# Batch 1's exp(q) transposed in quarters of the array, in one block ahead of its first kv

## The chip, the cores and the metric

One core of one Trainium2 chip. The metric is the device time of one execution in microseconds (us), the median of several runs; lower is better. A ratio given here is the mean time of one kernel's runs over that of the other's of the same rounds, so it is not quite the ratio of the medians that stand beside it.

## The reference

```python
# q, k, v: (8 batches, 8 heads, 576 rows, 64)
q_s = softmax(q, axis=-1)                  # over the 64
k_s = softmax(k, axis=2)                   # over the 576 rows
kv  = einsum('bhsd,bhse->bhde', k_s, v)        # 64 x 64 per head
x   = einsum('bhsd,bhde->bhse', q_s, kv)   # -> (4608, 512)
out = gelu(x @ w_in) @ w_out               # w_in 512x2048, w_out 2048x512
```

## The kernel before

TensorE does the matmuls and transposes, VectorE, ScalarE and GpSimd the work on single elements (exp, sums, casts, copies), and SyncE's queue issues nearly all of the loads. TensorE writes its results into banks of PSUM, from where VectorE or ScalarE copies them. TensorE works through the batches: transposes of exp(q), kv, x, then the two large products h (with w_in) and y (with w_out). Batch 1's attention is laid into the y stage of batch 0, which runs in 16 steps t of four matmuls each; step t needs row block t of w_out, cast to bf16.

```python
def tp_mm(b, half):                 # 8 full 128x128 transposes
    ...
    for i in range(2):
        hp = 2 * half + i
        for j in range(J):
            nc.tensor.transpose(ps[:, j, i, :], <eq of two heads, 128 x 128>, identity)

def norm_q(b, i=0, n=1, eng=None):  # half of the heads: sum, reciprocal, product
    ...
    nc.vector.reduce_sum(out=qsum, in_=eq[:, :, hs, :], axis=AX.X)
    nc.vector.reciprocal(recq, qsum)
    eng.tensor_tensor(out=eq[...], in0=eq[...], in1=<recq>, op=ALU.mult)
...
load_main(1, "q", q, 2)             # one queue, in this order
load_pair(1, "k", k, 2)
wo.append(load_wo(3))               # rows 12 and 13 of w_out
for hp in range(2):
    load_v1(hp)
load_wo_row(wo[3], 2)               # rows 14, 15
load_wo_row(wo[3], 3)
load_v1(2)
load_v1(3)
...
exp_q(1, parts=2)                   # ScalarE
exp_k(1, parts=2)
...
norm_q(1, 0, 2)                     # product on GpSimd
norm_q(1, 1, 2, nc.vector)          # product on VectorE
cast_wo(3, wo[3], 0, 2)             # rows 12 and 13, VectorE
for hp in range(HP):
    cast_v(1, hp, nc.gpsimd)
for t in range(12):
    y_part(t, range(J))
tp_step(1, 0)                       # transposes, copies on VectorE
tp_step(1, 1)
load(3)
cast_wo(3, wo[3], 2, 1, "s")        # row 14, ScalarE
cast_wo(3, wo[3], 3, 1, "s")        # row 15
y_part(12, range(J))
y_part(13, range(J))
kv_mm(1, 0)                         # 36 matmuls in 64x64 quarters
kv_norm(1, 0)
y_part(14, range(J))
y_part(15, (0, 1))
...
x_mm(1, 0)                          # 4 matmuls in quarters
kv_mm(1, 1)
```

The softmax here doesn't subtract the row's maximum and nothing guards it: scores larger than these inputs give would overflow.

Of the kernel before, what the change touches and what calls it, by code (L numbers as in the profile page):

```python
# [9 lines left out]
BF16 = mybir.dt.bfloat16  # L10
# [6 lines left out]
def kernel(  # L17
# [16 lines left out]
    nc = tc.nc  # L34
# [3 lines left out]
    J = 4  # L38
    M = 128 * J
    R = S - M  # L40
    HP = H // 2
# [8 lines left out]
    attn_sb = ctx.enter_context(tc.tile_pool(name="attn_sb", bufs=2))  # L50
    small = ctx.enter_context(tc.tile_pool(name="small", bufs=4))
    moe_sb = ctx.enter_context(tc.tile_pool(name="moe_sb", bufs=4))
    psum_h = ctx.enter_context(tc.tile_pool(name="psum_h", bufs=3, space=bass.MemoryType.PSUM))
    psum_y = ctx.enter_context(tc.tile_pool(name="psum_y", bufs=2, space=bass.MemoryType.PSUM))
    psum_a = ctx.enter_context(tc.tile_pool(name="psum_a", bufs=1, space=bass.MemoryType.PSUM))

    identity = singles.tile([128, 128], BF16)
# [20 lines left out]
    def table(func):  # L78
        nc.scalar.activation(out=scr[:, 1:2], in_=scr[:, 0:1], func=func)  # L79

    st = [dict() for _ in range(B + 1)]
# [30 lines left out]
    def load(b):  # L112
        load_main(b, "q", q)
        load_pair(b, "k", k)
        load_pair(b, "v", v)
# [52 lines left out]
    def kv_tiles(b):  # L168


        if b == 0:
            p = [psum_h.tile([128, 512], FP32, tag="h", name="kv")[:, 0:256] for i in range(2)]
            ps = psum_a.tile([128, 4, 256], FP32, tag="a2", name="kv")
            st[b]["kvall"] = ps[:, 0::2]
            p += [ps[:, 0, :], ps[:, 2, :]]
        else:
            ps = psum_a.tile([128, 4, 256], FP32, tag="a2", name="kv")
            st[b]["kvall"] = ps
            p = [ps[:, i, :] for i in place]
        st[b]["kv"] = p  # L180
# [7 lines left out]
    def kv_mm(b, half):  # L188


        if "kv" not in st[b]:
            kv_tiles(b)
        for n in range(NS):
            for i in range(2):
                for hh in range(2):
                    hp = 2 * half + i
                    pr = slice(hh * 64, hh * 64 + 64)
                    c = slice((hh ^ i) * 64, (hh ^ i) * 64 + 64)
                    nc.tensor.matmul(  # L199
                        st[b]["kv"][hp][c, 0:D + 1], ek[b % 2][pr, hp, n, :],  # L200
                        v_aug[b % 2][pr, hp, n, 0:D + 1], start=(n == 0), stop=(n == NS - 1),
                    )

    def kv_norm(b, half=None):

        ps = st[b]["kvall"]
        if half is None:
            parts = [(ps, kvc[b], 4)]
        elif b == 0 and half == 0:
            parts = [(st[b]["kv"][hp].unsqueeze(1), kvc[b][:, hp:hp + 1], 1) for hp in range(2)]  # L210
        elif b == 0:
            parts = [(ps, kvc[b][:, 2:4], 2)]
        else:
            parts = [(ps[:, 1:3] if half == 0 else ps[:, 0::3], kvc[b][:, 2 * half:2 * half + 2], 2)]
        for src, dst, m in parts:
            rec = small.tile([128, 4], FP32, tag="reck")
            nc.vector.reciprocal(rec[:, 0:m], src[:, :, D])
            nc.vector.tensor_tensor(  # L218
                out=dst, in0=src[:, :, 0:D],
                in1=rec[:, 0:m].unsqueeze(2).to_broadcast([128, m, D]), op=ALU.mult,  # L220
            )
# [6 lines left out]
    def norm_q(b, i=0, n=1, eng=None):  # L228

        eng = eng or nc.gpsimd  # L230
        eq = st[b]["eq"]
        w = H // n
        hs = slice(i * w, (i + 1) * w)
        qsum = small.tile([128, J, w], FP32, tag="qsum")
        recq = small.tile([128, J, w], FP32, tag="recq")
        nc.vector.reduce_sum(out=qsum, in_=eq[:, :, hs, :], axis=AX.X)  # L236
        nc.vector.reciprocal(recq, qsum)  # L237
        eng.tensor_tensor(  # L238
            out=eq[:, :, hs, :], in0=eq[:, :, hs, :],
            in1=recq.unsqueeze(3).to_broadcast([128, J, w, D]), op=ALU.mult,  # L240
        )

    def tp_mm(b, half):
        if half == 0:
            st[b]["qT"] = attn_sb.tile([128, J, HP, 128], BF16, tag="qT", name="qT")
        if b == 1 and half == 1:
            ps = psum_a.tile([128, 2, J, 2, 128], BF16, tag="a2", name="tp")[:, 0]
        else:
            pool, tag = (psum_h, "h") if half == 1 else (psum_a, "a")
            ps = pool.tile([128, J, 2, 128], BF16, tag=tag)  # L250
        st[b][f"tp{half}"] = ps
        for i in range(2):
            hp = 2 * half + i
            for j in range(J):
                nc.tensor.transpose(  # L255
                    ps[:, j, i, :],
                    st[b]["eq"][:, j, 2 * hp:2 * hp + 2, :].rearrange("p h d -> p (h d)"),
                    identity,
                )

    def tp_evac(b, half, eng="v"):
        o = st[b]["qT"][:, :, 2 * half:2 * half + 2, :]
        if eng == "v":
            nc.vector.tensor_copy(out=o, in_=st[b][f"tp{half}"])
        else:
            nc.scalar.copy(out=o, in_=st[b][f"tp{half}"])

    def tp_step(b, half):
        tp_mm(b, half)
        tp_evac(b, half)  # L270

    def xbar_step(b):
        st[b]["qT"] = attn_sb.tile([128, J, HP, 128], BF16, tag="qT", name="qT")
# [80 lines left out]
    def y_mm(c, ps, j, t):  # L354
        nc.tensor.matmul(  # L355
            ps, st[c]["g"][:, t, j * 128:(j + 1) * 128], wo_bf[:, t, :],
            start=(t == 0), stop=(t == NDF - 1),
        )
# [83 lines left out]
    def load_wo(i):  # L442
        w = wst.tile([128, 4, DM], FP32, tag="w")
        src = moe_w_out[i * 512:(i + 1) * 512, :]
        if i == 0:
            for h in range(2):
                nc.sync.dma_start(
                    out=w[:, 2 * h:2 * h + 2],
                    in_=src[256 * h:256 * h + 256].rearrange("(p c) f -> p c f", c=2),
                )  # L450
            return w
        src = src.rearrange("(p c) f -> p c f", c=4)
        if i == 3:
            nc.sync.dma_start(out=w[:, 0:2], in_=src[:, 0:2])
            return w
        nc.sync.dma_start(out=w, in_=src)
        return w
# [5 lines left out]
    def cast_wo(i, w, c0=0, n=4, eng="v"):  # L463
        o, w = wo_bf[:, 4 * i + c0:4 * i + c0 + n, :], w[:, c0:c0 + n]
        if eng == "v":
            nc.vector.tensor_copy(out=o, in_=w)
        else:
            nc.scalar.copy(out=o, in_=w)
# [18 lines left out]
    wo = [load_wo(i) for i in range(3)]  # L487
# [19 lines left out]
    norm_q(0, 0, 2)  # L507
    norm_q(0, 1, 2, nc.vector)
    tp_mm(0, 0)
    cast_v(0, 0, nc.scalar)  # L510
    cast_v(0, 1, nc.scalar)
# [3 lines left out]
    x_tile(0, 0, psum_y, "y")  # L515
    x_tile(0, 1, psum_y, "y")
    tp_mm(0, 1)
    tp_evac(0, 1, "s")
    x_tile(0, 2, psum_a, "a")
# [40 lines left out]
    exp_k(1, parts=2)  # L560
    table(AF.Gelu)
    cast_wo(2, wo[2])
    yps = [psum_h.tile([128, DM], FP32, tag="h", name="ps") for j in range(2)]
    yps += [psum_y.tile([128, DM], FP32, tag="y", name="ps") for j in range(2)]
    norm_q(1, 0, 2)
    norm_q(1, 1, 2, nc.vector)
    cast_wo(3, wo[3], 0, 2)
    for hp in range(HP):
        cast_v(1, hp, nc.gpsimd)

    def y_part(t, js):
        for j in js:
            y_mm(0, yps[j], j, t)

    for t in range(12):
        y_part(t, range(J))
    tp_step(1, 0)
    tp_step(1, 1)
    load(3)
    cast_wo(3, wo[3], 2, 1, "s")  # L580
    cast_wo(3, wo[3], 3, 1, "s")
    y_part(12, range(J))
    y_part(13, range(J))
    kv_mm(1, 0)
    kv_norm(1, 0)
    y_part(14, range(J))
    y_part(15, (0, 1))
# [110 lines left out]
```

## Time and profile before

| | before |
|---|---|
| time, median | 279.49 us (279.39 to 279.51, 3 runs) |
| TensorE busy | 97% of 277.7 us |
| granted clock | 0.998 |
| DMA engines, first 48.6 us | busy for nine tenths or more in six of the seven slices of 6.9 us, at 397 to 429 GB/s |

The table says: TensorE's stream sets the time, and for nearly all of the first 48 us the loads keep the DMA engines full beside it.

### The profile page before, as it was taken

How to read it: one execution, taken by the hardware profiler on the slowest of the kernel's cores; microseconds unless marked ns; L12 is line 12 of the kernel's file. 1: busy time of each engine (PE TensorE's matmuls, PEld its weight loads, DVE VectorE, ACT ScalarE, POOL GpSimd, SP SyncE). 2: the span in 40 equal slices, each digit the busy share in tenths (PEclk: the TensorE clock that was granted, in tenths of full speed). 3: DMA queues.
4: the chain of work that ended last, by engine and by line, in shares of the span. 5: the costliest groups of instructions: out<-in, count | busy, mean ns of one | idle time of the engine just before them, and what ended most of it. 6: DMA issues, size and time to landing. Idle time of an engine off the chain costs nothing.

```text
span 277.7 us, 4535 instructions
## 1 busy us (share of the span) xinstructions
PE 269.6 (97%) x1890; PEld 126.3 (45%) x1918; DVE 100.7 (36%) x154; ACT 157.8 (57%) x246; POOL 32.4 (12%) x26
## 2 busy tenths in 40 slices
PE   7899999999999999999999999999999999999995
PEld 3444454444444444444444444444444444444443
DVE  2876574319753540093008400751015200130012
ACT  4867675789377717791669246943683363126400
POOL 1520051002020220004000500050005000000000
PEclk9999999999999999999999999999999999999999
DMA  7999999964992248712981199017401500220033
GB/s 254 397 401 429 399 400 407 400 245 107 305 328 59 75 104 256 288 38 91 251 340 40 47 254 380 34 46 193 112 0 76 151 2 0 76 78 0 0 78 77
DMA packets 44980, 50.10 MB, mean 180 GB/s; under 512 B 20384, under 2 KB 29856, under 8 KB 44704
## 3 DMA queue, kind: packets, MB, share of 16 engines
q1 hardware_dynamic: 44560, 49.39, 53.0%
q10 hardware_dynamic: 400, 0.43, 0.6%
q8 instruction: 15, 0.25, 0.4%
q14 instruction: 5, 0.04, 0.1%
HBM read 36.70 MB, written 9.44 MB: 166 GB/s over the span
## 4 chain that ended last, share of the span: by engine, by line
PE 93%; DMA 4%; issue 1%; POOL 0%; DVE 0%; SPq 0%
PE ps L327 44%; PE ps L355 43%; DMA f<-in_v_dram 2%; PE kv L199 2%; PE ps L294 2%; DMA f<-in_q_dram 1%; PE ps L380 1%; PE pair L327 1%; POOL v_aug L162 0%; PE ps L299 0%; PE tp L255 0%; PE ps L255 0%; SPq L103 0%; DVE kvc L218 0%; DVE y_sb L385 0%
## 5 line engine op out<-in xcount | busy, mean ns | idle before, releaser
L327 PE MATMUL ps<-xT,wi_bf 128*128 128x512 bf16 x557 | 124.2, 379 | 0.5
L355 PE MATMUL ps<-wo_bf,g 128*128 128x512 bf16 x543 | 122.1, 379 | 1.6 <-issue 1.1
L333 ACT ACTIVATE g<-ps 128x512 bf16<-128x512 f32 x142 | 83.5, 598 | 66.8 <-PE ps L327 66.8
L327 PEld LDWEIGHTS <-wi_bf 128*128 128x128 bf16 x576 | 56.1, 98 | 68.0 <-POOL wi_bf L440 0.2
L355 PEld LDWEIGHTS <-g 128*128 128x128 bf16 x560 | 53.8, 98 | 64.4 <-issue 0.4
L363 DVE COPY y_sb<-ps 128x512 f32<-128x512 f32 x33 | 22.6, 684 | 82.1 <-PE ps L355 79.1
L238 POOL TENSOR_TENSOR e<-e,recq 128x2048 bf16<-128x2048 bf16 (+1 forms) x9 | 25.7, 2855 | 176.3 <-DVE recq L237 141.7
L162 DVE CAST v_aug<-f 128x576 bf16<-128x576 f32 x24 | 16.4, 745 | 47.6 <-DMA f<-in_v_dram 47.6
L236 DVE TENSOR_REDUCE qsum<-e 128x16 f32<-128x1024 bf16 (+1 forms) x13 | 21.1, 1622 | 14.2 <-ACT e L145 14.2
L320 ACT CAST xT<-ps 128x512 bf16<-128x512 f32 x18 | 9.9, 588 | 28.4 <-PE ps L294 18.3
L145 ACT ACTIVATE e<-f 128x512 bf16<-128x512 f32 (+1 forms) x42 | 20.5, 556 | 3.3 <-DMA f<-in_q_dram 3.2
L150 ACT ACTIVATE ek<-f 128x2304 bf16<-128x2304 f32 (+1 forms) x10 | 17.2, 1728 | 0.7 <-DMA f<-in_k_dram 0.7
L318 DVE CAST xT<-ps 128x512 bf16<-128x512 f32 x17 | 11.0, 686 | 16.8 <-PE ps L294 14.0
L79 ACT ACT_TABLE_LOAD x9 | 11.5, 1283 | 2.8 <-issue 2.6
L473 PE MATMUL ps<-zeros 128*128 128x512 f32 x14 | 9.0, 814 | 1.5 <-DVE zeros L498 1.5
L145 ACT ACT_TABLE_LOAD x7 | 9.0, 1283 | 0.1
L199 PEld LDWEIGHTS <-ek 64*64 64x64 bf16 x576 | 6.5, 105 | 2.7 <-issue 1.0
L432 DVE CAST wi_bf<-w 128x512 bf16<-128x512 f32 x12 | 6.9, 616 | 1.9 <-DMA w<-in_moe_w_in_dram 1.6
L199 PE MATMUL kv<-v_aug,ek 64*64 64x65 bf16 x576 | 7.0, 193 | 0.5 <-POOL v_aug L162 0.5
L473 PEld LDWEIGHTS ps<-zeros 128*128 128x128 f32 x14 | 3.6, 269 | 6.0 <-issue 4.5
L238 DVE TENSOR_TENSOR e<-e,recq 128x1024 bf16<-128x1024 bf16 x4 | 6.2, 1550 | 0.1
L294 PE MATMUL ps<-qT,kvc 64*64 64x512 bf16 x62 | 5.4, 390 | 0.5 <-DVE kvc L218 0.4
(38 smaller groups left out, 49.8 us busy)
## 6 DMA issues: line engine op xcount, KB each, us to landing
out_dram<-y_sb SPq DMA_DIRECT2D x32, 256.0 KB, 2.4
f<-in_k_dram SPq DMA_DIRECT2D x6, 1152.0 KB, 10.2
f<-in_v_dram SPq DMA_DIRECT2D x6, 1152.0 KB, 11.6
f<-in_q_dram SPq DMA_DIRECT2D x6, 1024.0 KB, 7.0
w<-in_moe_w_in_dram SPq DMA_DIRECT2D x6, 512.0 KB, 8.4
f<-in_v_dram SPq DMA_DIRECT2D x8, 288.0 KB, 6.5
f<-in_q_dram SPq DMA_DIRECT2D x4, 512.0 KB, 8.8
w<-in_moe_w_out_dram SPq DMA_DIRECT2D x2, 1024.0 KB, 12.1
```

The lines of the kernel that those rows point to most:

```text
L79: nc.scalar.activation(out=scr[:, 1:2], in_=scr[:, 0:1], func=func)
L145: nc.scalar.activation(out=dst[:, i], in_=src[:, u], func=AF.Exp)
L150: nc.scalar.activation(out=ek[b % 2][:, i:i + n], in_=st[b]["kf"][:, i:i + n].rearrange("p x (n d) -> p x n d", n=NS), func=AF.Exp,)
L162: eng.tensor_copy(out=o, in_=i)
L199: nc.tensor.matmul(st[b]["kv"][hp][c, 0:D + 1], ek[b % 2][pr, hp, n, :], v_aug[b % 2][pr, hp, n, 0:D + 1], start=(n == 0), stop=(n == NS - 1),
L236: nc.vector.reduce_sum(out=qsum, in_=eq[:, :, hs, :], axis=AX.X)
L238: eng.tensor_tensor(out=eq[:, :, hs, :], in0=eq[:, :, hs, :], in1=recq.unsqueeze(3).to_broadcast([128, J, w, D]), op=ALU.mult,)
L327: nc.tensor.matmul(ps, wi_bf[:, dm, t * 128:(t + 1) * 128], st[c]["xT"][:, dm, :], start=(dm == 0), stop=(dm == NDM - 1),)
L333: nc.scalar.activation(out=st[c]["g"][:, t, :], in_=ps, func=AF.Gelu)
L355: nc.tensor.matmul(ps, st[c]["g"][:, t, j * 128:(j + 1) * 128], wo_bf[:, t, :], start=(t == 0), stop=(t == NDF - 1),)
L363: nc.vector.tensor_copy(out=y_sb, in_=ps)
L473: nc.tensor.matmul(ps, z[:, 0:128], z, start=True, stop=True)
```

## The change

Its intent: the transposes are made in the four quarters of the array, as kv is, and put next to kv, so that both form one block in one tiling mode. Each half of the partitions gets its own PSUM bank; VectorE copies one, ScalarE the other. Since y step 12 now comes before the transposes, the cast of row 12 is split from row 13's. (The diff is cut; left out is also the branch of tp_mm that gave the old second tile its bank.)

```diff
+    def tp_quarters(b, tps):
+        for hp in range(HP):
+            for j in range(J):
+                for hh in range(2):
+                    for r in range(2):
+                        pr = slice(r * 64, r * 64 + 64)
+                        nc.tensor.transpose(
+                            tps[r][hh * 64:hh * 64 + 64, hp, j, :],
+                            st[b]["eq"][pr, j, 2 * hp + hh, :], identity[pr, pr],
+                        )
+    def tp_quarters_evac(b, tps, r, eng):      # cut: one copy on VectorE or ScalarE
...
+    tps = [pool.tile([128, HP, J, 64], BF16, tag=tag, name="tp")
+           for pool, tag in ((psum_a, "a"), (psum_h, "h"))]
...
-    cast_wo(3, wo[3], 0, 2)
+    cast_wo(3, wo[3], 0, 1)
+    cast_wo(3, wo[3], 1, 1)
...
-    tp_step(1, 0)
-    tp_step(1, 1)
     load(3)
...
     y_part(12, range(J))
     y_part(13, range(J))
+    tp_quarters(1, tps)
     kv_mm(1, 0)
+    tp_quarters_evac(1, tps, 0, "v")
+    tp_quarters_evac(1, tps, 1, "s")
     kv_norm(1, 0)
```

More of the change, by code (lines that the diff above doesn't have):

```diff
@@ L245, in tp_mm @@
             st[b]["qT"] = attn_sb.tile([128, J, HP, 128], BF16, tag="qT", name="qT")
-        if b == 1 and half == 1:
-            ps = psum_a.tile([128, 2, J, 2, 128], BF16, tag="a2", name="tp")[:, 0]
-        else:
-            pool, tag = (psum_h, "h") if half == 1 else (psum_a, "a")
-            ps = pool.tile([128, J, 2, 128], BF16, tag=tag)
+        pool, tag = (psum_h, "h") if half == 1 else (psum_a, "a")
+        ps = pool.tile([128, J, 2, 128], BF16, tag=tag)
         st[b][f"tp{half}"] = ps
@@ L266, in tp_evac @@
             nc.scalar.copy(out=o, in_=st[b][f"tp{half}"])
-    def tp_step(b, half):
-        tp_mm(b, half)
-        tp_evac(b, half)
+    def tp_quarters(b, tps):
[9 more added lines that the diff above has]
+    def tp_quarters_evac(b, tps, r, eng):
+        if r == 0:
+            st[b]["qT"] = attn_sb.tile([128, J, HP, 128], BF16, tag="qT", name="qT")
+        o = st[b]["qT"].rearrange("p j x m -> p x j m")[:, :, :, r * 64:r * 64 + 64]
+        if eng == "v":
+            nc.vector.tensor_copy(out=o, in_=tps[r])
+        else:
+            nc.scalar.copy(out=o, in_=tps[r])
     def xbar_step(b):
```

## The prediction

> **What bounds the kernel now.** I first read the busy shares and the heads of the chain of waits on the page, to see which engine's time is the kernel's time.
>
> ```profile
> PE 269.6 (97%) x1890; PEld 126.3 (45%) x1918; DVE 100.7 (36%) x154; ACT 157.8 (57%) x246; POOL 32.4 (12%) x26
> ...
> PE 93%; DMA 4%; issue 1%; POOL 0%; DVE 0%; SPq 0%
> ```
>
> TensorE is busy 97% of the 277.7 us span and holds 93% of the chain that ended last; the 4% of DMA lie in the first 11 us. The granted clock is 0.998. So from 12.7 us on, time taken from TensorE's stream comes off the end one for one, as long as no other engine becomes late by it.
>
> Next I read the chain of waits in order of time around batch 1's front end, which the change touches. Columns: start in us, length in us, what. A piece runs from the end of the work before it to its own end, so its length is what it adds to the chain.
>
> ```profile
> 38.44 0.45 PE ps L255 x8
> 38.89 0.45 PE tp L255 x8
> 39.34 1.73 PE ps L355 x8
> 41.06 0.41 PE kv L199 x36
> 41.47 0.32 PE ps L355
> 41.79 0.05 issue
> 41.85 1.02 PE ps L355 x4
> 42.87 0.34 PE ps L294 x4
> 43.21 0.34 PE kv L199 x34
> 43.55 0.54 PE ps L355 x2
> ```
>
> L255 are the transposes of exp(q), L355 the output matmuls (y), L199 kv, L294 the attention product x. There is no wait in it: 16 full transposes add 0.90 us (56 ns each), eight y matmuls 1.73 (216 each), the first half of kv 0.41.
>
> The same chain, near its end, holds the one block that is nearly the new one's shape: 64 matmuls of 64x64 weights and 64 columns, entered from full-array matmuls.
>
> ```profile
> 241.80 0.67 PE ps L299 x64
> ```
>
> Last I read the timeline of ScalarE, VectorE and GpSimd in the same stretch, for the slack of what will stand after the transposes. Columns: start, length, engine, line, operation.
>
> ```profile
> 39.73 1.28 ACT L468 CAST wo_bf<-w 128x512 bf16<-128x512 f32 x2 [0.82 <-DMA w<-in_moe_w_out_dram]
> 43.26 0.58 ACT L320 CAST xT<-ps 128x512 bf16<-128x512 f32 x1 [2.25 <-PE ps L294]
> ...
> 36.22 1.68 DVE L238 TENSOR_TENSOR e<-e,recq 128x1024 bf16<-128x1024 bf16 x1
> 37.82 0.68 DVE L466 CAST wo_bf<-w 128x1024 bf16<-128x1024 f32 x1
> ...
> 39.53 0.68 DVE L264 COPY qT<-tp 128x1024 bf16<-128x1024 bf16 x1
> 41.54 0.17 DVE L217 RECIPROCAL rec<-kv 128x2 f32<-128x2 f32 x1 [1.32 <-PE kv L199]
> 41.74 0.29 DVE L218 TENSOR_TENSOR kvc<-kv,rec 128x128 bf16<-128x128 f32 x1
> ```
>
> ScalarE stands idle from 41.01 to 43.26 and VectorE from 40.21 to 41.54: the two copies of the new order have room there.
>
> **What the Trainium skill says.** "TensorEngine Tiling (Array Packing)", section Key Properties: tiles of one mode run independently and in parallel, but a change of the mode drains the engine. The trace agrees in size: 36 kv matmuls entered from full-array work add 0.41 us, 36 that follow x in the same mode add 0.34, so entry costs about 0.07. The same page, section Gotcha 1: row tiles must not write one PSUM bank at the same time; the change gives each half of the partitions its own bank. "TensorE: Matmul & The Clock Gate", Part 4, tells of some 275 ns for a transpose in a kernel, with the full clock not engaging. The trace has 219 ns for one, but 56 ns from one to the next, so in a stream they run at the full rate; the measurement decides. "VectorE: DVE Perf Modes", section Mode 2x_1P, says that 16-bit elements go two per cycle where neighbours are packed and aligned. The trace agrees: 1024 bf16 out of PSUM took 0.68 us, as long as 512 fp32 (the y_sb copies, 0.68).
>
> **The change part by part.**
>
> Removed: 16 full transposes ahead of y step 12, 0.90 us on the chain.
>
> Added: 64 transposes of 64x64, right ahead of the first kv. With kv they form one block in one mode, so no mode change is added: the entry moves from kv to the transposes. Steady rate in this mode: 36 kv in 0.34 us are 9.4 ns each, and the x block of 64 gives (0.67 - 0.07)/64 = 9.4. So the block costs 64 x 9.4 + 0.07 = 0.67 us, the measured length of L299, and the kv after it loses its entry: 0.34 instead of 0.41. I chose these as models because operand sizes, the alternation of row halves and the 64-column stream are nearly the same; what is untested is the transpose mode.
>
> Sum on TensorE, from the end of y step 11 to the end of kv: before 0.90 + 1.73 + 0.41 = 3.04 us; after 1.73 + 0.67 + 0.34 = 2.74. **A gain of 0.30 us.**
>
> Moved, and whether it stays hidden (times shifted by that gain):
> - y step 12 now follows step 11 directly, at 38.44 instead of 39.34, and needs row 12 of w_out. That cast is split in two. Casts of this kind cost (1.23 - 0.68)/1024 = 0.54 ns an element, so one row takes about 0.40 us and, started at 37.82, is ready near 38.25. The first matmul of step 12 enters the array about 38.25 (its piece ends 216 ns after 38.44). A tie, worth 0.1 us at most; unsplit, the cast would have cost about 0.3. The second row, near 38.65, has till 39.1.
> - Transposes then end near 40.84 and kv near 41.18. VectorE copies one half from 40.9 to about 41.6 (0.69), then the reciprocal and product (0.46): kv is normalised near 42.1. The x matmuls start about 42.3 (their piece, now 42.57 to 42.91, less some 0.3 for their own passage). Slack 0.2 us.
> - ScalarE ends its two casts at 41.01 and copies the other half in about 1.01 us, the time of the one such copy it made for batch 0: done near 42.05. Slack again some 0.25 us. The x products now need both copies, where they needed VectorE's alone.
> - PSUM banks: the built program gives the second transpose tile the bank that the last GELU of the stage before frees; the first y matmuls keep their banks and waits, so allocating it earlier blocks nothing.
> - kv's second half needs two v casts of GpSimd that end at 42.44; it would start at 42.9. Hidden.
>
> Everything later is the same stream 0.30 us earlier.
>
> **The rivals.**
> 1. A new wait takes the gain. The copies now stand between the transposes and x with only 0.2 us to spare. VectorE's writes change to runs of 64 elements; should this halve its rate, 1024 elements would take about 0.68 + 512 x 1.04 ns = 1.2 us (slope my estimate, twice the 0.54 of the casts less fixed cost), kvc comes near 42.6 and x waits some 0.3: time unchanged, near 279.5. For it: slack is small. Against: runs of 64 remain packed.
> 2. The transposes do not overlap between quarters. At a full-array rate for 64 columns, half the 56 ns, 64 take 1.8 us, 1.1 more than planned, and the copies end later too: about 280.5. For it: no transpose in this trace runs in quarters. Against: kv and x do, with nearly the same shape and bank pattern.
> 3. The gain is hidden anyway, because a load or cast sets a later start. The DMA engines are full in this stretch (some 390 to 410 GB/s), and w_out's last rows and batch 1's v land just ahead of their use. Against: after 12.7 us the chain has no DMA in it, and slack of the nearest, GpSimd's v casts, is 0.5 us. It would leave 279.3 to 279.5.
>
> **Range and chances.** 279.49 - 0.30 = 279.19; a little of rivals 1 and 3 and the tie of step 12 bring it to 279.2. The runs before lie within 0.12 us. The low end, 278.95, is the gain plus noise and a somewhat faster block; the high end, 279.6, holds a gain wholly eaten and noise. I give the overlap about nine chances in ten. Two per cent is 5.6 us, which nothing here comes near: within 2% at 0.98, 0.01 to either side.
>
> **What the changed profile would show.** Right: in the chain, y steps 10 to 13 unbroken, then 64 transposes in about 0.67 us and 36 kv in 0.34 with no issue gap between; the x matmuls near 42.57 without a wait; VectorE's copy still near 0.7 us, ScalarE's near 1.0. Wrong: a piece of VectorE or ScalarE (qT, kvc) in the chain before x means rival 1; transposes adding 25 ns or more each, rival 2; a DMA or GpSimd piece after 43 us, rival 3. A wait of y step 12 on the w_out cast would show the tie lost. A time above 279.6 means that one of them took more than the whole gain.

## More of the kernel before

The timeline of TensorE (start, length, engine, line, work, and in brackets the idle time before it with what ended it):

```profile
27.92 10.52 PE L355 MATMUL ps<-wo_bf,g 128*128 128x512 bf16 x47
```

```profile
31.98 1.24 ACT L145 ACTIVATE e<-f 128x512 bf16<-128x512 f32 x3 [1.97 <-DMA f<-in_q_dram]
```

TensorE begins y at 27.92; twelve steps of four matmuls at 0.216 us each are fed to it till 38.28, where the transposes start. ScalarE waits for batch 1's q and begins its exp when it lands, at 31.98. VectorE does two sums, two reciprocals, one product and then the cast of rows 12 and 13. In this kernel nothing on TensorE needs that cast before 39.17.

## The result, and the profile after

| | before | changed |
|---|---|---|
| time, median | 279.53 us (279.39 to 279.65, 6 runs) | 279.57 us (279.24 to 279.88, 6 runs) |
| span of the profiled run | 277.7 us | 277.7 us |

The ratio is 1.0002, interval 0.9989 to 1.0015: the same time. The forecast gain of 0.30 us did not come. Parts of the chain of waits of the changed kernel, from the load of q to x, say where it went; lines of the source have moved by 14 (y is L369, x L308), and the new transposes are L272.

```profile
19.80 12.47 DMA f<-in_q_dram
...
36.50 1.70 DVE e L238
38.20 0.35 DVE wo_bf L480
38.55 0.04 issue
38.59 1.89 PE ps L369 x8
40.47 0.64 PE tp L272 x64
41.11 0.35 PE kv L199 x33
...
42.87 0.34 PE ps L308 x4
```

Before, the chain kept to TensorE from 12.7 us on, but for 0.5 us of VectorE at 13.2 us and the last copy. Now it runs back from y step 12 over VectorE's cast of row 12, its product on exp(q), the sums and the exp to the load of q, and TensorE enters it only at 38.59. The block that was built is there and costs what was forecast: 64 transposes 0.64 us and kv 0.35. The timeline of TensorE shows the wait itself.

```profile
27.76 10.52 PE L369 MATMUL ps<-wo_bf,g 128*128 128x512 bf16 x47
38.59 1.89 PE L369 MATMUL ps<-wo_bf,g 128*128 128x512 bf16 x8 [0.30 <-DVE wo_bf L480]
```

The account closes. In this execution y began at 27.76, 0.16 earlier than in the trace of before. Twelve steps of four matmuls take 10.36 us (27.92 to 38.28 in the trace of before), so step 12 could have started at 38.12; it started at 38.59, 0.47 late. (The 0.30 in the bracket counts from the modelled end of the last matmul, which lies past the end of its feed.) The block's own saving, against the four pieces of before, is 0.45 + 0.45 + 1.73 + 0.41 - (1.73 + 0.64 + 0.35) = 0.32. And 0.16 + 0.32 - 0.47 is nothing: x starts at 42.80 in both traces. Why the cast was late, the timelines of ScalarE and VectorE tell; the first line of each is what came of q's landing, the second the new copy.

```profile
32.29 1.24 ACT L145 ACTIVATE e<-f 128x512 bf16<-128x512 f32 x3 [2.43 <-DMA f<-in_q_dram]
...
41.20 1.01 ACT L284 COPY qT<-tp 128x1024 bf16<-128x1024 bf16 x1
```

```profile
38.12 0.75 DVE L480 CAST wo_bf<-w 128x512 bf16<-128x512 f32 x2
41.17 0.69 DVE L282 COPY qT<-tp 128x1024 bf16<-128x1024 bf16 x1 [2.30 <-PE tp L272]
```

q landed 0.31 us later than in the trace of before (32.29 against 31.98), and everything behind it shifted by as much. SyncE's queue, which issues the loads in order, tells where these 0.31 us come from (before, then changed):

```profile
19.51 1.59 SPq L90 DMA_DIRECT2D f<-in_q_dram  x2
```

```profile
19.80 1.60 SPq L90 DMA_DIRECT2D f<-in_q_dram  x2
```

The load of q was issued 0.29 us later. From issue to the start of the exp it took 12.47 and 12.49 us, as good as the same. So the load itself was not slower; it started later. What it waited for, by the chain, is a load of w_in that landed at 19.78.

The two copies took 0.69 and 1.01 us as forecast, and x did not wait for them.

### The profile page after: what moved, and what is told of

The parts are those of the page before. It is cut to its first block, busy times and chain, and to the rows that moved or that the text cites. A ratio compares the mean times of both kernels' runs of the same rounds, so it can differ in the third digit from the quotient of the medians. Undisturbed runs are those within 1.5% of the kernel's fastest.

```text
span 277.7 us, 4630 instructions
## 1 busy us (share of the span) xinstructions
PE 269.1 (97%) x1938; PEld 126.0 (45%) x1966; DVE 100.6 (36%) x154; ACT 158.9 (57%) x247; POOL 32.5 (12%) x26
## 4 chain that ended last, share of the span: by engine, by line
PE 84%; DMA 11%; DVE 2%; issue 1%; ACT 0%; SPq 0%
PE ps L369 40%; PE ps L341 40%; DMA f<-in_q_dram 6%; DMA w<-in_moe_w_in_dram 3%; DMA f<-in_v_dram 2%; PE kv L199 2%; PE ps L308 1%; PE ps L394 1%; DVE qsum L236 1%; DVE e L238 1%; ACT e L145 0%; PE ps L313 0%; PE tp L272 0%; DVE recq L237 0%; DVE wo_bf L480 0%
## 5 line engine op out<-in xcount | busy, mean ns | idle before, releaser
L369 PE MATMUL ps<-wo_bf,g 128*128 128x512 bf16 x543 | 122.1, 379 | 1.9 <-issue 1.1
L369 PEld LDWEIGHTS <-g 128*128 128x128 bf16 x560 | 54.0, 98 | 65.0 <-issue 1.0
L308 PE MATMUL ps<-qT,kvc 64*64 64x512 bf16 x62 | 5.6, 390 | 0.3 <-DVE kvc L218 0.2
```

The costliest lines, as they stand in the source:

```text
L369: nc.tensor.matmul(ps, st[c]["g"][:, t, j * 128:(j + 1) * 128], wo_bf[:, t, :], start=(t == 0), stop=(t == NDF - 1),)
```

## The experiments

**Theories.** A: the gain on TensorE is real, and y step 12, moved forward, turns it into a wait for the cast of row 12, which stands on VectorE behind its work on q and so hangs on the landing of q. B: the loads hold the whole stretch, so that without this wait the next one takes its place. C: the late landing was chance, and typical runs do gain. The kernels ran in three groups, each on one chip beside nine common runs of before: after_again, skip_row12, one_cast and early_row12 (before: 279.49 us, 279.39 to 279.59); moved_full, quarters_early, before_early and early_v_act (279.61, 279.42 to 280.01); before_again, pool_norm and early_v_again (279.54, 279.35 to 279.68). Each kernel was timed five times.

| run | median, us | ratio to before | 95% interval |
|---|---|---|---|
| before_again | 279.55 | 0.9999 | 0.9986 to 1.0011 |
| after_again | 279.55 | 1.0004 | 0.9991 to 1.0016 |
| skip_row12 | 279.18 | 0.9994 | 0.9981 to 1.0006 |
| one_cast | 280.14 | 1.0021 | 1.0009 to 1.0034 |
| early_row12 | 279.34 | 0.9992 | 0.9978 to 1.0006 |
| moved_full | 279.87 | 1.0007 | 0.9994 to 1.0019 |
| quarters_early | 279.38 | 0.9989 | 0.9976 to 1.0003 |
| before_early | 279.79 | 1.0008 | 0.9995 to 1.0020 |
| early_v_act | 279.22 | 0.9988 | 0.9976 to 1.0001 |
| early_v_again | 279.21 | 0.9987 | 0.9973 to 1.0000 |
| pool_norm | 280.11 | 1.0023 | 1.0010 to 1.0035 |

Only the intervals of one_cast and pool_norm, both slower, leave out 1. That a kernel here is faster than before by 0.1 to 0.4 us is shown by its trace, not by the times.

### The two kernels again: before_again and after_again

No edit (a comment at the end of the file).

> The kernel before against itself: how far two sets of runs of one kernel differ (expected: ratio within 0.0005 of 1), and a second trace of it: the cast of rows 12 and 13 again done well ahead of step 12 (by 0.5 us or more), no wait of TensorE between 30 and 43 us, or at most one of the second half of the transposes on VectorE's product when q lands late.

> The changed kernel once more, as control and as a second look at how late the loads are. Theory A (the gain of 0.30 us on TensorE is eaten by y step 12, which now waits for the cast of row 12 of w_out at the end of VectorE's work on batch 1's q): same time as before within 0.1 us, about 279.5, and again a VectorE piece for the cast ahead of y step 12 in the chain, 0.1 to 0.5 us of wait depending on when q lands. Theory C (the first runs had late loads by chance): 279.2 and no wait.

Measured: before against itself gives 0.9999, so no offset between two sets of runs shows here, though the interval is ten times that. Its second trace again has no wait, and the cast of rows 12 and 13 ended at 38.45, 0.78 us ahead of its step 12. The changed kernel's second trace has y begun at 27.92, so that step 12 could start at 38.28; it started at 38.62, 0.34 late, again behind VectorE's cast. With two traces of two that have the wait, and medians of 279.57 and 279.55, theory C falls: single runs may gain (279.24 and 279.32 are among the eleven), the typical one does not.

### Step 12 without its cast: skip_row12

```diff
-            ps, st[c]["g"][:, t, j * 128:(j + 1) * 128], wo_bf[:, t, :],
+            ps, st[c]["g"][:, t, j * 128:(j + 1) * 128],
+            wo_bf[:, 11 if c == 0 and t == 12 else t, :],
```

Its output is wrong, which doesn't matter for the time. Relative error 0.12: step 12 uses a row that was cast long before.

> Wrong result on purpose: y step 12 of batch 0 multiplies by row block 11 of w_out, cast long before, so that it has no cast to wait for; every instruction and duration is kept. Theory A: y steps 11, 12, 13 unbroken, time 0.3 us below before, about 279.2. Theory B (the loads hold this stretch in several places, and the next wait takes over: step 13's row, the normalised exp(q), v's casts or rows 14 and 15): time stays at 279.5 and the chain shows another VectorE, GpSimd or ScalarE piece before 43 us.

```profile
32.88 7.34 PE ps L369 x34
40.22 0.64 PE tp L272 x64
40.85 0.35 PE kv L199 x35
41.21 1.40 PE ps L369 x6
42.61 0.34 PE ps L308 x4
```

The chain of waits is one unbroken run of y matmuls, and x is done 0.26 us earlier than before's (x began at 42.54, against 42.80) although y began 0.04 later. (By the 6.3 us that step 12 follows the start of the exp in the changed kernel, 38.59 - 32.29, its cast would here have let it start near 38.5, with the exp at 32.19, some 0.2 after TensorE was ready.) The median is 279.18, 0.31 below before. Four of the five runs lie between 279.14 and 279.24; the fifth took 279.88, which no trace explains and which alone brings the ratio up to 0.9994. Theory A holds, and B does not, as far as this wait goes.

### A longer cast: one_cast

```diff
-    cast_wo(3, wo[3], 0, 1)
-    cast_wo(3, wo[3], 1, 1)
+    cast_wo(3, wo[3], 0, 2)
```

> The changed kernel with the cast of rows 12 and 13 in one instruction again, as before the change. Theory A: step 12 waits until the whole cast, 0.68 instead of 0.41 us, is done: 0.3 us more wait, time about 279.8. If the cast were not what holds the end: no change, 279.5.

```profile
32.78 1.25 ACT e L145 x3
...
38.69 0.62 DVE wo_bf L480
39.30 0.04 issue
39.35 1.89 PE ps L369 x8
```

The chain shows the cast's piece at 0.62 instead of 0.35, as forecast, and step 12 right behind it. The median rose by 0.59 over after_again, more than the 0.3 expected. In the trace 0.27 us come from the cast and 0.45 from q, which landed at 32.78 instead of 32.33. Whether q is later in this kernel by rule or was so in this run, one trace can't tell; two of the five runs (279.86 and 279.88) lie where the cast alone would put them. Either way the end follows the cast.

### The cast out of the way, with a right result: early_row12

```diff
-    load_pair(1, "k", k, 2)
-    wo.append(load_wo(3))
+    load_pair(1, "k", k, 2, lambda: wo.append(load_wo(3)))    # between the two halves of k
...
-    norm_q(1, 1, 2, nc.vector)
-    cast_wo(3, wo[3], 0, 1)
-    cast_wo(3, wo[3], 1, 1)
+    norm_q(1, 1, 2, nc.vector, lambda: cast_wo(3, wo[3], 0, 2))  # ahead of the product
...
-    cast_wo(3, wo[3], 2, 1, "s")
-    cast_wo(3, wo[3], 3, 1, "s")
+    cast_wo(3, wo[3], 2, 1)
+    cast_wo(3, wo[3], 3, 1)
```

(load_pair and norm_q were given a parameter that calls the lambda at these places.)

> Right result. Rows 12 and 13 of w_out are loaded between the two halves of batch 1's k and cast by VectorE ahead of its product on exp(q), not after it; rows 14 and 15 are cast by VectorE, not ScalarE, as exp(k)'s second half now ends 1.3 us later on ScalarE. Theory A: cast ready near 37.3, step 12 unbroken, time 279.2, 0.3 below before. Theory B: a later wait, most likely of the transposes on the product (ends near 38.9, needed near 39.9) or of step 14 or 15 on rows 14 and 15, gives it back: 279.5.

```profile
40.20 0.64 PE tp L276 x64
...
42.60 0.34 PE ps L312 x4
42.94 0.49 PE kv L201 x36
```

```profile
41.52 1.38 POOL L164 CAST v_aug<-f 128x576 bf16<-128x576 f32 x2 [1.28 <-DMA f<-in_v_dram]
```

y runs unbroken to 40.20 although q landed late (32.42), and x starts 0.27 us earlier than before's, at 42.53. But kv's second half then takes 0.49 us instead of 0.34: GpSimd's last cast of v ends at 42.90, and this kv, now early, waits for it. So B holds in part: behind the wait that was removed stands a second one, worth 0.15 us. The median is 0.15 below before, which fits the 0.3 less that, but lies inside the interval. The early cast was not free: it took 1.28 us instead of 0.68 while GpSimd's product ran beside it (till 37.24), and was ready at 37.79, not at 37.3; it was still in time.

### The last cast of v on ScalarE: early_v_act and early_v_again

early_row12, and

```diff
-    for hp in range(HP):
+    for hp in range(HP - 1):
         cast_v(1, hp, nc.gpsimd)
...
     tp_quarters_evac(1, tps, 1, "s")
+    cast_v(1, HP - 1, nc.scalar)
```

> The early version, with the last of batch 1's four casts of v on ScalarE after its copy of qT, where GpSimd's ended at 42.90 and held kv's second half by 0.15 us. Theory A: that cast is done by about 42.6, or when v's last part lands, near 42.2, plus 0.6: kv's second half is back at 0.34 us and the time at 279.2, 0.15 below the early version. If v's landing is the limit, the wait stays at 0.1 or so and nothing is gained.

> The early version with v's last cast on ScalarE once more, beside the null control: theory A 279.2, 0.25 to 0.3 below before; wait of kv's second half for v's last part 0 to 0.15 us according to its landing.

```profile
42.32 0.67 ACT L162 CAST v_aug<-f 128x576 bf16<-128x576 f32 x1 [0.40 <-DMA f<-in_v_dram]
```

The wait did not go: kv's second half spans 0.78 and 0.73 us on the timeline, against 0.67 in early_row12 and 0.51 in before. The line is of early_v_act; ScalarE sat idle until v landed. The last part of v landed at 42.32 and 42.19, and ScalarE's cast takes 0.67, so it is ready at 43.0 and 42.9, where GpSimd's was at 42.90. The second branch of the expectation is the right one: v's landing is the limit, not the engine. The times, 279.22 and 279.21, are the lowest of a correct kernel here, 0.39 and 0.33 below before (ratios 0.9988 and 0.9987, upper ends of the intervals at 1.0001 and 1.0000). As the trace gives no reason for their being 0.12 below early_row12, that difference is best taken for noise. The profiled runs, of which the traces are, took 279.47 and 279.34.

### The two halves of the change: moved_full and quarters_early

moved_full makes the old full transposes in the new place, into the new banks:

```diff
-    tp_quarters(1, tps)
+    tp_mm(1, 0)
+    tp_mm(1, 1)
     kv_mm(1, 0)
```

(The tiles have the old shape, and tp_evac copies one on VectorE, the other on ScalarE.)

> The move alone: the 16 full transposes of before, in the new place (between y step 13 and the first kv), into the same two banks, with the split cast and the copies shared by VectorE and ScalarE; no quarters. Theory A: the block of transposes and first half of kv adds 0.90 + 0.41 us to the chain where the quarters and kv add 0.99, and step 12 still waits 0.2 to 0.5 us for its cast: about 279.8, 0.3 above the changed kernel. If the quarters bring nothing, 279.5 as the changed kernel.

quarters_early makes the new transposes in the old place, ahead of step 12, with both copies on VectorE:

```diff
     for t in range(12):
         y_part(t, range(J))
+    tp_quarters(1, tps)
+    tp_quarters_evac(1, tps, 0, "v")
+    tp_quarters_evac(1, tps, 1, "v")
...
     y_part(13, range(J))
-    tp_quarters(1, tps)
     kv_mm(1, 0)
```

> The quarters alone: 64 transposes of 64x64 in the old place, ahead of y step 12, copied by VectorE as before. Theory A: TensorE is occupied while the cast of row 12 finishes, so step 12 has no wait; the block costs about 0.64 plus 0.1 for a second change of mode, y 1.73, kv 0.41: 2.9 us from step 11 to the end of kv against 3.04 before, 0.1 to 0.15 gained, about 279.4. If the transposes of heads 4 to 7 come too early for VectorE's product (ends 37.9 to 38.2), a wait of up to 0.1 takes that too and the time is before's, 279.5.

The chain of moved_full, then that of quarters_early:

```profile
40.31 0.89 PE tp L252 x16
41.20 0.41 PE kv L199 x36
```

```profile
38.51 0.64 PE tp L272 x64
39.15 1.83 PE ps L369 x8
40.98 0.41 PE kv L199 x36
```

From the end of step 11 to the end of kv, waits left out, TensorE takes 3.04 us in before (prediction), 1.73 + 0.89 + 0.41 = 3.03 in moved_full, 0.64 + 1.83 + 0.41 = 2.88 in quarters_early and 1.73 + 0.64 + 0.35 = 2.72 in the full change. So the move alone brings nothing on TensorE, the quarters alone 0.16, and standing next to kv another 0.16, because one exit (0.10 on the y steps) and one entry (0.06 on kv) fall away. quarters_early has no wait, as the transposes fill the time in which the cast finishes, and came out at 279.38, 0.23 below before (inside the interval). moved_full had no wait in its trace either, since q landed early (32.12) and y began late (28.05); its median of 279.87 is what its missing gain and a wait in other runs would give, but those runs have no trace.

### Two that did not do what they were made for: before_early and pool_norm

before_early gives the kernel before the load order and casts of early_row12.

> The kernel before with the early load and cast of rows 12 and 13 and rows 14 and 15 on VectorE, transposes as before. Theory A: before does not wait for that cast, so this brings it nothing: 279.5 within 0.1, step 12 still starts right after the transposes. If it were faster by 0.2 us or more, the gain of the early version would come from the loads and not from the quarters.

Its median is 0.18 above before, inside the interval, so there is no sign that the gain of the early version comes from the loads. But it isn't a clean control: the second eight transposes start 0.67 us after the first eight instead of 0.45, because VectorE's product, now behind the cast, ended only at 38.79. (The chain names exp(k)'s second half, which ended at 38.94. The first weights of these transposes were loaded at 38.91, before that, so it was the product.) These 0.22 us are the whole of its delay in the trace: x starts at 43.02 instead of 42.80. So apart from them the early loads neither gained nor lost.

pool_norm takes the product on heads 4 to 7 off VectorE:

```diff
-    norm_q(1, 1, 2, nc.vector)
+    norm_q(1, 1, 2)
```

> The changed kernel with the product on heads 4 to 7 of exp(q) on GpSimd instead of VectorE, so that the cast of row 12 no longer stands behind it; loads in the old order, right result. Theory A: the cast starts when its rows land, near 37.6 to 37.9, and is done near 38.2: the wait falls from 0.3 to 0.5 us to 0 to 0.1, time about 279.25. GpSimd's product ends near 39.1, so its casts of v end 0.4 later, near 40.5, still ahead of kv (40.7 to 40.9). If v's casts become late for kv, a GpSimd piece shows there and the time is 279.5.

```profile
34.81 3.76 POOL L238 TENSOR_TENSOR e<-e,recq 128x1024 bf16<-128x1024 bf16 x2 [19.61 <-DVE recq L237]
```

```profile
37.36 2.29 DVE L480 CAST wo_bf<-w 128x512 bf16<-128x512 f32 x2 [1.31 <-DMA w<-in_moe_w_out_dram]
```

A miss: 280.11. The rows landed at 37.36 as expected and VectorE took up the casts, but the two took 2.29 us instead of 0.75; the first was done only at 38.86 by the chain, after GpSimd's product ended at 38.57 (34.81 + 3.76). The Trainium skill, "SBUF — State Buffer", section Who interferes with whom, says that VectorE and GpSimd share a pair of SBUF ports, that casts can take it, and that the later of the two is blocked until the earlier has finished. The two lines agree with it. The cast was taken out from behind one instruction and put behind the same instruction on another engine.

## Why the prediction was right or wrong

The time lay in the range (279.57 in 278.95 to 279.60), but the forecast median, 279.2, was not reached; the whole gain was eaten. That the range held is no credit to the mechanism: its upper end had been set to hold "a gain wholly eaten and noise". Point by point:

- **The cost of the block: right.** Forecast 0.67 for the transposes and 0.34 for kv; measured 0.64 and 0.35. L299 was a good model for transposes in quarters, and rival 2 (no overlap between quarters) is out.
- **One mode change for both: right.** moved_full and quarters_early split the measured 0.32 into 0.16 for the quarters and 0.16 for the exit and entry saved.
- **Copies and kv's norm hidden: right.** 0.69 and 1.01 us; the packed rate was kept, x did not wait. Rival 1 as it was put (copies, qT, kvc) is out.
- **Banks: right.** No y matmul waits at 27.8 us. (No run let both halves write one bank, so that rule of the skill is not tested here.)
- **The move of step 12, "a tie, worth 0.1 us at most": wrong.** This is the step that failed. The duration in it was right (a row's cast: forecast 0.40 us, measured 0.41). What was wrong was to take VectorE's start times of one trace as fixed. They hang on when q lands. Over the 13 traces the exp of q began between 31.88 and 32.78 us, and before's 31.98 was among the three earliest. In the changed kernel step 12 starts 6.3 us after that (38.59 - 32.29, 38.62 - 32.33), and TensorE, with y begun at 27.92, is ready at 38.28. So a landing at 31.98 gives the tie exactly, and one at 32.3 costs 0.3. The wait was 0.47 and 0.34 in the two traces, against the 0.1 allowed; of the 0.47, 0.31 are q's later landing and 0.16 TensorE's earlier start. The prediction had named its own sign for this, a wait of y step 12 on the w_out cast, and the sign came. What moves is the issue of the load: it lies between 19.37 and 20.27 us in the 13 traces, and the exp follows it by 12.47 to 12.52 us in all of them.
- **Rival 3, "a load sets a later start", is what happened,** through VectorE's cast, and it was argued away with "after 12.7 us the chain has no DMA in it". That view shows only what held the end before; it says nothing of how far behind the loads were. The slack of 0.5 us given there for GpSimd's casts of v was misread too: it takes kv's start from the chain (43.21, the end of the work before it), where the timeline has 43.04. Less the gain of 0.30, that leaves 42.74 - 42.44 = 0.30 us, and in early_row12 it was used up.

What stays open: the one long run of skip_row12, and why the issue of q's load differs by 0.9 us between traces. In all 13 it falls within 0.02 us of VectorE's start on a part of w_in that has just landed (19.80 and 19.80 in the changed kernel's first trace), so the lateness of that earlier load is handed on; where it comes from, no run asks. Both traces of before have q early (31.98, 31.94) and both of the changed kernel late (32.29, 32.33); but pool_norm and quarters_early, whose loads are the changed kernel's, have it at 31.88 and 32.05, so the change does not always delay it. Whether it does on the average, 13 traces can't tell, and it is an open rival: in the ten traces of the changed kernel and those built on it, the load of w_out ahead of q's is done issuing only at 19.1 us or later, in the three of before and before_early by 18.7. The changed kernel's times (279.24 to 279.97 over 11 runs) spread wider than before's in the same rounds (279.39 to 279.65). That this comes from q's landing is argued, as only the profiled runs have traces; and before itself reached 280.01 in one other group.

## What to carry to other kernels

When work is taken out from in front of an instruction, that instruction moves forward on the clock, and each thing it needs must be early enough for the new time; check that with the latest landing seen, not with the one in a single trace. Where loads run at their full rate beside the bound engine, a gain smaller than the spread of their landings is worth only what their slack allows, so look for an order in which the bound engine has other work while the late operand arrives (here quarters_early), or bring the operand forward (here early_row12). Quarter-array work of different kinds is worth putting side by side: here half of the saving came from the neighbour.

## What the Trainium skill lacked or had wrong

- "TensorEngine Tiling (Array Packing)", Key Properties, says that a change of the mode drains the engine and gives no cost: here some 0.06 us going in (kv 0.41 against 0.35) and 0.10 coming out (y steps 12 and 13, 1.83 against 1.73).
- "TensorE: Matmul & The Clock Gate", Part 4, has no rate for a stream of transposes and says that the full clock does not engage: here, between matmuls and at a granted clock of 1.00, 16 full ones took 0.90 us, 56 ns each (a quarter of a y matmul, with a quarter of its columns, is 54), and 64 in quarters 0.64 us, 10 ns each with the entry. A long stretch of transposes alone was not run.
- No page that I read tells how far a load's start moves between executions when the DMA engines are full: here 0.90 us (issue at 19.37 to 20.27), while the time from issue to the landing stayed within 0.05 us (12.47 to 12.52, up to the start of the exp that waits for it).
